# FFN in groups of up to four units, with q and k transposed together: a fused retention and FFN kernel on one core

## The chip, the core and the metric

The kernel runs on one core of a Trainium2 chip. The core has a matrix engine (TensorE, in the profile PE, its weight loads PEld), a vector engine (DVE), an activation engine (ACT), GpSimd (POOL) and a sync engine (SP) that issues DMAs here. Each engine works through its own instructions in order and waits on semaphores for the others. The metric is the device time of one execution in microseconds, as the median of several runs.

## What is computed

Eight batches of eight heads, 576 positions of 64 numbers. Scores are scaled, multiplied by a causal decay of each head, and applied to v; the result of all heads is one row of 512 per token, which goes through an FFN of 512 to 2048 to 512 with a squared ReLU.

```python
scores = scale * np.matmul(q, k.transpose(0, 1, 3, 2))
gamma = 1.0 - 2.0 ** (-5.0 - np.arange(H, dtype=np.float32))
rel = pos[:, None] - pos[None, :]
Dmat = np.where(rel >= 0, gamma[:, None, None] ** rel[None, :, :], 0.0)
ret = scores * Dmat[None, :, :, :]
attn_out = np.matmul(ret, v).astype(np.float32)
x = np.ascontiguousarray(attn_out.transpose(0, 2, 1, 3)).reshape(B * S, H * D)
h = x @ w_in
r = np.maximum(h, 0.0)
out = ((r * r) @ w_out).astype(np.float32)
```

## The kernel before

The tokens are cut into 36 units of 128. A full unit is 128 positions of one batch; a tail unit holds the last 64 positions of two batches. Each unit goes through two stages.

The retention stage (`add_ret`) casts k, q and v to fp16 (k and v on POOL, q on DVE for the first four units and on POOL after that; v is multiplied by its decay into `vp`). PE transposes k and q into one PSUM tile `psT` (line 307): four transposes for the k part (`tk`), four for q (`tq`). ACT copies the two halves of k out into `kTb` (`fe0`, line 316, and `fe1`, line 319), DVE copies q into `qT` (line 323). PE makes the scores `psc` (line 375), DVE masks them into `rT` (line 383). The state of earlier chunks, `R`, is made from `psS` (line 336) by DVE (`stmp`, line 350, then `R`, line 355, with the decay `bdec`). PE adds the two contributions into `psO` (lines 407 and 411), and DVE multiplies by the decay `gam` into `xT` (line 423).

The FFN stage (`add_ff`) multiplies `xT` by w_in: 16 output blocks of four accumulating matmuls, each with 128 moving columns (line 441, called FF1 below), four blocks to a PSUM bank `ph`. ACT takes the ReLU of a bank into `rl` (line 450), DVE squares it into `gT` (line 455). Sixteen accumulating matmuls with 512 moving columns then give `po` (line 466, FF2), which ACT copies out to `o` (line 474) and stores.

The order is not written out by hand. `Schedule` is a planner: each task has an engine, a key (smaller goes first among those that are ready), an estimated duration, the tasks it needs and the buffers it takes. `emit` plays the tasks through in the planner's own time and emits the instructions in the order that comes out. Constants are built ahead of it, so on DVE and POOL they stand before every task. The planner counts two banks for `ph` and one for `po`; both come from one pool of three.

Loads come from SP in one chain: k, q, v of units 0 to 3, then w_in and w_out in four pieces of 1 MB each (five stage buffers), then k, q, v of the other units. Each weight piece is cast in halves, one on DVE and one on ACT (line 256). The five load buffers of k, q and v are freed by the casts.

Of the kernel before, what the change touches and what calls it, by code (L numbers as in the profile page):

```python
# [97 lines left out]
def kernel(  # L98
# [26 lines left out]

    const = ctx.enter_context(tc.tile_pool(name="const", bufs=1))
    ld = ctx.enter_context(tc.tile_pool(name="ld", bufs=5))
    stage = ctx.enter_context(tc.tile_pool(name="stage", bufs=5))
# [26 lines left out]
    for h in range(H):  # L155
        nc.vector.memset(lnrow[:, h:h + 1], -lng[h])
    lncol = const.tile([P, NP], FP32, name="lncol")
# [3 lines left out]
    lnscale = const.tile([P, 1], FP32, name="lnscale")  # L161
    nc.vector.memset(lnscale, math.log(scale))

    mask = {}
    for kind in ("full", "tail"):
# [5 lines left out]
    nc.gpsimd.memset(mask["tail"][0:64, 64:128], 0.0)  # L171

    iota_pt = const.tile([P, 1], FP32, name="iota_pt")
    nc.vector.tensor_copy(out=iota_pt[0:64], in_=iota_p[0:64])
    nc.vector.tensor_scalar(out=iota_pt[64:128], in0=iota_p[64:128], scalar1=-64.0, scalar2=None, op0=ALU.add)
    vdec = {}
    for kind, pos in (("full", iota_p), ("tail", iota_pt)):
        t = const.tile([P, H], FP32, name=f"vdl_{kind}")
        nc.vector.tensor_scalar(out=t, in0=lnrow, scalar1=pos, scalar2=None, op0=ALU.mult)
        d = const.tile([P, H], FP32, name=f"vdec_{kind}")  # L180
        nc.scalar.activation(out=d, in_=t, func=ACTF.Exp, bias=lnscale, scale=1.0)
        vdec[kind] = d
    gam_f = const.tile([P, NP, P], FP32, name="gam_full")
    gam_t = const.tile([P, NP, P], FP32, name="gam_tail")
    for hp in range(NP):
        nc.scalar.activation(out=gam_f[:, hp, :], in_=iota_f, func=ACTF.Exp, scale=lncol[:, hp:hp + 1])  # L186
    nc.vector.tensor_copy(out=gam_t[:, :, 0:64], in_=gam_f[:, :, 0:64])
    nc.vector.tensor_copy(out=gam_t[:, :, 64:128], in_=gam_f[:, :, 0:64])
    gam = {"full": gam_f, "tail": gam_t}

    bdec = const.tile([P, NP, P], FP32, name="bdec")
    nc.vector.memset(bdec, 0.0)
    for hp in range(NP):
        nc.vector.memset(bdec[0:64, hp, 0:64], math.exp(128.0 * lng[2 * hp]))
        nc.vector.memset(bdec[64:128, hp, 64:128], math.exp(128.0 * lng[2 * hp + 1]))
# [299 lines left out]
    for u in range(NU):  # L495
        add_ff(u)
# [31 lines left out]
```

## Time and profile before

| | |
|---|---|
| median of 3 runs | 355.31 us (353.95 to 356.13) |
| the profiled execution | 354.32 us |
| its span | 352.6 us |
| instructions in the span | 9372 |
| PE matmul busy | 325.5 us (92%), 4000 matmuls |
| PE weight load busy | 250.7 us (71%) |
| DVE busy | 192.4 us (55%) |
| ACT busy | 155.3 us (44%) |
| POOL busy | 83.3 us (24%) |
| HBM read, written | 36.70 MB, 9.44 MB |

Busy time is the time that an engine's instructions cover. A matmul's busy time runs until its modelled end, so matmuls that follow each other overlap in the table of groups, and the spacing of their starts is what they cost in a stream. The profile's slices show the span in 40 parts, each digit a busy share in tenths. The timeline merges like instructions that follow each other; its columns are start, duration, engine, line, operation, and in brackets the idle time before it with what ended it. A row of the DMA slices and of the stretches gives the mean share of 16 DMA engines.

### The profile page before, as it was taken

How to read it: one execution, taken by the hardware profiler on the slowest of the kernel's cores; microseconds unless marked ns; L12 is line 12 of the kernel's file. 1: busy time of each engine (PE TensorE's matmuls, PEld its weight loads, DVE VectorE, ACT ScalarE, POOL GpSimd, SP SyncE). 2: the span in 40 equal slices, each digit the busy share in tenths (PEclk: the TensorE clock that was granted, in tenths of full speed). 3: DMA queues.
4: the chain of work that ended last, by engine and by line, in shares of the span. 5: the costliest groups of instructions: out<-in, count | busy, mean ns of one | idle time of the engine just before them, and what ended most of it. 6: DMA issues, size and time to landing. Idle time of an engine off the chain costs nothing.

```text
span 352.6 us, 9372 instructions
## 1 busy us (share of the span) xinstructions
PE 325.5 (92%) x4000; PEld 250.7 (71%) x4000; DVE 192.4 (55%) x400; ACT 155.3 (44%) x267; POOL 83.3 (24%) x117
## 2 busy tenths in 40 slices
PE   0479999999999999999999999999999999999994
PEld 0478857777777777777777777777777777777772
DVE  5689635554455555555455555555455555555440
ACT  3137843444434444444444444444444444444441
POOL 4400264422222222223122222222122222100000
PEclk9999999999999999999999999999999999999999
DMA  9999999998955444444445454555521000000001
GB/s 173 235 387 386 271 232 235 237 211 181 219 137 120 111 109 115 119 122 121 121 121 121 119 121 121 122 121 122 120 61 32 32 32 32 30 32 33 32 32 31
DMA packets 122026, 46.75 MB, mean 133 GB/s; under 512 B 113280, under 2 KB 113280, under 8 KB 121984
## 3 DMA queue, kind: packets, MB, share of 16 engines
q1 hardware_dynamic: 116736, 36.71, 45.4%
q10 hardware_dynamic: 5248, 9.44, 8.2%
q8 instruction: 31, 0.51, 0.6%
q14 instruction: 11, 0.09, 0.1%
HBM read 36.70 MB, written 9.44 MB: 131 GB/s over the span
## 4 chain that ended last, share of the span: by engine, by line
PE 86%; ACT 6%; DVE 4%; issue 1%; DVEq 0%
PE ph L441 34%; PE po L466 33%; PE psT L307 6%; ACT kTb L316 5%; PE psc L375 5%; PE psO L407 5%; PE psS L336 2%; PE psO L411 2%; DVE stmp L350 1%; DVE rT L383 1%; DVE w_in L256 0%; DVE R L355 0%; ACT kTb L319 0%; ACT gam_full L186 0%; DVE kTb L206 0%
## 5 line engine op out<-in xcount | busy, mean ns | idle before, releaser
L441 PE MATMUL ph<-xT,w_in 128*128 128x128 f16 x2304 | 158.3, 219 | 0.7 <-DVE w_in L256 0.7
L466 PE MATMUL po<-w_out,gT 128*128 128x512 f16 x576 | 155.0, 379 | 0.0
L441 PEld LDWEIGHTS <-w_in 128*128 128x128 f16 x2304 | 139.4, 98 | 9.6 <-DVE w_in L256 1.1
L450 ACT ACTIVATE rl<-ph 128x512 f16<-128x512 f32 x144 | 85.3, 596 | 53.5 <-PE ph L441 53.3
L455 DVE TENSOR_TENSOR gT<-rl 128x512 f16<-128x512 f16 x144 | 65.3, 456 | 37.6 <-ACT rl L450 37.2
L466 PEld LDWEIGHTS <-gT 128*128 128x128 f16 x576 | 53.3, 98 | 36.3
L474 ACT COPY o<-po 128x512 f32<-128x512 f32 x36 | 21.1, 586 | 97.2 <-PE po L466 93.9
L283 POOL CAST q<-q 128x512 f16<-128x512 f32 x32 | 19.8, 619 | 103.8 <-PE psT L307 60.0
L383 DVE TENSOR_TENSOR rT<-psc,mask_full 128x512 f16<-128x512 f32 x64 | 41.2, 682 | 4.3 <-PE psc L375 4.3
L288 POOL TENSOR_TENSOR vp<-v,vdec_full 128x512 f16<-128x512 f32 x32 | 34.2, 1069 | 36.2 <-PE psO L411 23.7
L407 PEld LDWEIGHTS <-vp 128*128 128x128 f16 x288 | 28.2, 100 | 19.3 <-issue 0.4
L375 PE MATMUL psc<-qT,kTb 128*128 128x128 f16 x288 | 38.4, 226 | 1.7 <-DVE qT L323 1.7
L279 POOL CAST k<-k 128x512 f16<-128x512 f32 x36 | 23.3, 647 | 70.5 <-DMA k<-in_k_dram 31.6
L407 PE MATMUL psO<-rT,vp 128*128 128x128 f16 x288 | 39.5, 224 | 0.0
L350 DVE TENSOR_TENSOR stmp<-psS,R 128x512 f32<-128x512 f32 x24 | 16.6, 690 | 38.4 <-PE psS L336 38.4
L423 DVE TENSOR_TENSOR xT<-psO,gam_full 128x512 f16<-128x512 f32 x32 | 22.1, 691 | 21.5 <-PE psO L411 18.0
L323 DVE COPY qT<-psT 128x512 f16<-128x512 f16 x36 | 15.3, 424 | 31.6 <-ACT rl L450 27.5
L319 ACT COPY kTb<-psT 64x512 f16<-64x512 f16 x36 | 20.9, 580 | 20.5 <-DVE qT L323 15.2
L316 ACT COPY kTb<-psT 64x512 f16<-64x512 f16 x36 | 20.8, 578 | 20.6 <-PE psT L307 20.1
L307 PEld LDWEIGHTS <-q 128*128 128x128 f16 x144 | 11.2, 99 | 24.2 <-issue 17.5
L307 PE MATMUL psT<-ident,q 128*128 128x128 f16 x144 | 14.4, 224 | 14.8 <-ACT kTb L316 6.8
L411 PE MATMUL psO<-qT,R 128*128 128x128 f16 (+1 forms) x128 | 24.7, 215 | 0.0
(49 smaller groups left out, 144.0 us busy)
## 6 DMA issues: line engine op xcount, KB each, us to landing
k<-in_k_dram SPq DMA_DIRECT2D x32, 256.0 KB, 4.4
q<-in_q_dram SPq DMA_DIRECT2D x32, 256.0 KB, 4.7
v<-in_v_dram SPq DMA_DIRECT2D x32, 256.0 KB, 3.3
out_dram<-o ACTq DMA_DIRECT2D x32, 256.0 KB, 2.7
wi<-in_moe_w_in_dram SPq DMA_DIRECT2D x4, 1024.0 KB, 9.4
wo<-in_moe_w_out_dram SPq DMA_DIRECT2D x4, 1024.0 KB, 8.0
k<-in_k_dram SPq DMA_DIRECT2D x8, 128.0 KB, 4.3
q<-in_q_dram SPq DMA_DIRECT2D x8, 128.0 KB, 4.2
```

The costliest lines, as they stand in the source:

```text
L279: nc.gpsimd.tensor_copy(out=t, in_=tile_of["k32", u].rearrange("p h d -> p (h d)"))
L288: nc.gpsimd.tensor_tensor(out=vo, in0=tile_of["v32", u].rearrange("p (n a) d -> p n a d", a=2), in1=vdec[kind].rearrange("p (n a o) -> p n ...
L307: nc.tensor.transpose(tile_of["psT", u][:, i, hp, :], tile_of[src, u][:, hp * P:(hp + 1) * P], ident)
L316: nc.scalar.copy(out=kT[0:64, :, 0, :], in_=tile_of["psT", u][0:64, 0])
L375: nc.tensor.matmul(tile_of["psc", u, half][:, j, a, :], lhsT=kT[:, hp, a, :], rhs=tile_of["qT", u][:, hp, :], start=True, stop=True)
L383: nc.vector.tensor_tensor(out=tile_of["rT", u][:, 2 * half:2 * half + 2].rearrange("p n a i -> p (n a) i"), in0=tile_of["psc", u, half].re ...
L407: nc.tensor.matmul(ps[:, hp, :], lhsT=vps[u % NB][:, hp, a * 64:a * 64 + P], rhs=tile_of["rT", u][:, hp, a, :], start=(a == 0), stop=(a == ...
L411: nc.tensor.matmul(ps[:, hp, lo:hi], lhsT=tile_of["R", ru][:, hp, :], rhs=tile_of["qT", u][:, hp, lo:hi], start=False, stop=(n == len(inte ...
L441: nc.tensor.matmul(tile_of["ph", u, fb][:, j, :], lhsT=w_in16[:, m, fi * P:(fi + 1) * P], rhs=tile_of["x", u][:, m, :], start=(m == 0), st ...
L450: nc.scalar.activation(out=t, in_=tile_of["ph", u, fb], func=ACTF.Relu)
L455: nc.vector.tensor_tensor(out=t, in0=rl, in1=rl, op=ALU.mult)
L466: nc.tensor.matmul(tile_of["po", u], lhsT=tile_of["g", u, fi // 4][:, fi % 4, :], rhs=w_out16[:, fi, :], start=(fi == 0), stop=(fi == NF - 1))
```

## The change

It has five parts.

- FFN groups. The units are put into groups of 1, 1, 2, then seven of 4, then 2, 1, 1. A group of n units has one `xT` of n x 128 columns. FF1 runs once for a group, with n x 128 moving columns; a `ph` bank then holds 4/n output blocks. FF2 stays one unit at a time. FF1 of a group needs the `xT` part of its last unit. `gT` has 32 buffers instead of 16, `xT` three instead of five.
- Transposes. q's transposes have the key just behind k's. From unit 4 on both wait for both casts and share `psT`; the ACT copies wait for q's transposes, the second ACT copy for the first, and DVE's `qT` for the second ACT copy. For the first four units q's transposes go to a bank of the score pool instead.
- Constants as tasks. `bdec` is filled on POOL from an ACT exponential instead of on DVE. Zeroing of the buffer sets 1 to 3 of `vp` and `kTb`, and the mask, positions and decay of the tail units, move from DVE and the start to POOL tasks; DVE zeroes set 0 alone.
- TensorE is warmed up: a first task of 40 matmuls of the identity with itself.
- FFN banks. `ph` and `po` share a count of three banks. Four weight stage buffers instead of five. Two latencies and some durations of the planner have new numbers.

The core of the diff:

```diff
-    LAT = {"PE": 0.25, "ACT": 0.12, "DVE": 0.12, "POOL": 0.15, "SP": 2.0}
+    LAT = {"PE": 0.25, "ACT": 0.12, "DVE": 0.12, "POOL": 0.12, "SP": 2.1}
...
+    sizes = [1, 1, 2] + [4] * 7 + [2, 1, 1]
...
-    stage = ctx.enter_context(tc.tile_pool(name="stage", bufs=5))
+    stage = ctx.enter_context(tc.tile_pool(name="stage", bufs=4))
...
-    x_pool = ctx.enter_context(tc.tile_pool(name="x", bufs=5))
+    x_pool = ctx.enter_context(tc.tile_pool(name="x", bufs=3))
-    g_pool = ctx.enter_context(tc.tile_pool(name="g", bufs=16))
+    g_pool = ctx.enter_context(tc.tile_pool(name="g", bufs=32))
...
-    sched = Schedule(dict(ph=2, po=1, psc=2, psT=1, psS=1, psO=1, ld=5, wst=5, k16=4, q16=4,
-                          qT=3, rT=3, x=5, g=4, rl=3, o=2, R=6))
+    sched = Schedule(dict(ff=3, psc=2, psT=1, psS=1, psO=1, ld=5, wst=4, k16=4, q16=4,
+                          qT=3, rT=3, x=3, rl=3, o=2, R=6))
...
+    def warm():
+        ps = ps_ff.tile([P, P], FP32, name="warm", tag="ff")
+        for _ in range(40):
+            nc.tensor.matmul(ps, lhsT=ident, rhs=ident, start=True, stop=True)
+    add("PE", -1000, 5.5, warm)
+    zeroed = [[]]
+    for i in range(1, NB):
+        zeroed.append([add("POOL", -6 * L + L * i, 0.8, lambda i=i: (zero_kT(nc.gpsimd, i), zero_vp(nc.gpsimd, i)))])
+    def make_bdec():
+        nc.gpsimd.memset(bdec, 0.0)
+        for lo in (0, 64):
+            nc.gpsimd.tensor_copy(
+                out=bdec[lo:lo + 64, :, lo:lo + 64],
+                in_=dec128[lo:lo + 64].rearrange("p (n o) -> p n o", o=1).to_broadcast([64, NP, 64]))
+    made_bdec = add("POOL", -6 * L + 1, 1.1, make_bdec)
+    def make_tail_pool():
+        make_mask("tail")
...
+    tail_pool = add("POOL", 0, 2.2, make_tail_pool, deps=[made_bdec])
+    tail_dec = add("DVE", 0, 0.3, lambda: make_vdec("tail", tile_of["iota_pt"]), deps=[tail_pool])
...
-        tk = add("PE", base - 17.6, 0.22, ft(0, "k16"), deps=[ck], acq=("psT",))
-        tq = add("PE", base - 15.6, 0.22, ft(1, "q16"), deps=[cq, tk])
+        tk = add("PE", base - 17.6, 0.22, ft(0, "k16"), deps=[ck] if early else [ck, cq], acq=("psT",))
+        tq = add("PE", base - 17.5, 0.22, ft(1, "q16"), deps=[cq, tk], acq=("psc",) if early else ())
...
-        e0 = add("ACT", base - 15.5, 0.58, fe0, deps=[tk] + prev)
-        e1 = add("ACT", base - 15.4, 0.58, fe1, deps=[tk] + prev)
-        eq = add("DVE", base - 15.3, 0.42, feq, deps=[tq], acq=("qT",))
+        e0 = add("ACT", base - 15.5, 0.58, fe0, deps=[tk if early else tq] + prev)
+        e1 = add("ACT", base - 15.4, 0.58, fe1, deps=[e0])
+        eq = add("DVE", base - 15.3, 0.42, feq, deps=[tq] if early else [tq, e1], acq=("qT",))
...
-                        nc.tensor.matmul(tile_of["ph", u, fb][:, j, :], lhsT=w_in16[:, m, fi * P:(fi + 1) * P],
-                                         rhs=tile_of["x", u][:, m, :], start=(m == 0), stop=(m == NP - 1))
+                        nc.tensor.matmul(tile_of["ph", g, fb][:, j, :], lhsT=w_in16[:, m, fi * P:(fi + 1) * P],
+                                         rhs=tile_of["x", us[0]][:, m, :], start=(m == 0), stop=(m == NP - 1))
```

How the order changes at three places. First POOL at the start, where `k` is the fp16 cast of a unit's k and `vp` its v. Before:

```order
L167 MEMSET mask_full 128x128
L168 AFFINE_SELECT mask_full<-mask_full 128x128
L167 MEMSET mask_tail 128x128
L168 AFFINE_SELECT mask_tail<-mask_tail 128x128
L171 MEMSET mask_tail 64x64
L279 CAST k_189<-k_183 128x512
L288 TENSOR_TENSOR vp_163<-v_187,vdec_full 128x4x2x64
```

After, the rows from the end of the third buffer set on; ahead of them stand the mask, `bdec` and the first two sets:

```order
L207 MEMSET kTb_149 64x4x128
L208 MEMSET kTb_149 64x4x128
L204 MEMSET vp_145 128x4x64
L186 MEMSET mask_tail 128x128
L187 AFFINE_SELECT mask_tail<-mask_tail 128x128
L243 MEMSET mask_tail 64x64
L245 COPY iota_pt<-iota_p 64x1
L246 TENSOR_SCALAR iota_pt<-iota_p 64x1
L248 COPY gam_tail<-gam_full 128x4x64
L249 COPY gam_tail<-gam_full 128x4x64
L318 CAST k_226<-k_197 128x512
L327 TENSOR_TENSOR vp_142<-v_210,vdec_full 128x4x2x64
```

The first k cast moves behind all of POOL's constants. The second place is PE in the middle of the program, where one unit's k and q are transposed. Before:

```order
L307 MATMUL psT<-ident,k_984 128x128
L441 LDWEIGHTS w_in_96
L441 MATMUL ph<-xT,w_in_96 128x128
L441 LDWEIGHTS w_in_96
L441 MATMUL ph<-xT,w_in_96 128x128
L441 LDWEIGHTS w_in_96
L441 MATMUL ph<-xT,w_in_96 128x128
L441 LDWEIGHTS w_in_96
L441 MATMUL ph<-xT,w_in_96 128x128
L466 LDWEIGHTS gT
L466 MATMUL po<-w_out_97,gT 128x512
L307 LDWEIGHTS q_1014
```

After:

```order
L530 MATMUL po<-w_out_97,gT 128x512
L351 LDWEIGHTS k_1644
L351 MATMUL psT<-ident,k_1644 128x128
L351 LDWEIGHTS k_1644
L351 MATMUL psT<-ident,k_1644 128x128
L351 LDWEIGHTS k_1644
L351 MATMUL psT<-ident,k_1644 128x128
L351 LDWEIGHTS k_1644
L351 MATMUL psT<-ident,k_1644 128x128
L351 LDWEIGHTS q_1576
L351 MATMUL psT<-ident,q_1576 128x128
```

Four FF1 matmuls and one FF2 matmul stood between the two; now nothing does. The third place is ACT in the same stretch, where `kTb` are the two copies of k and `rl` a ReLU of FF1. Before:

```order
L474 COPY o<-po 128x512
L480 DMA out_dram<-o 128x512
L450 ACTIVATE rl<-ph 128x512 x3
L316 COPY kTb_180<-psT 64x4x128
L450 ACTIVATE rl<-ph 128x512
L319 COPY kTb_180<-psT 64x4x128
```

After:

```order
L511 ACTIVATE rl<-ph 128x512 x4
L357 COPY kTb_147<-psT 64x4x128
L360 COPY kTb_147<-psT 64x4x128
L511 ACTIVATE rl<-ph 128x512 x8
L357 COPY kTb_148<-psT 64x4x128
L360 COPY kTb_148<-psT 64x4x128
L511 ACTIVATE rl<-ph 128x512 x4
```

The ReLUs come sixteen to a group of four units, with the copies of two units between them, and the copies of the other two units fall into the group's FF2.

More of the change, by code (lines that the diff above doesn't have):

```diff
@@ L170 @@
         mask[kind] = m
[L171 to L182, printed above, removed]
+    make_mask("full")
@@ L270 @@
     T = {}
-    L = 2 * NF
     def add_ret(u):
         kind, b, c = units[u]
-        base = (u - 1) * L
+        us = groups[group_of[u]]
+        base = (u - len(us)) * L
+        early = u < ahead
+        tail = [tail_pool, tail_dec] if kind == "tail" else []
         def fk():
@@ L425, in add_ret, with add_ff @@
+        T["x", u] = add("DVE", base + 22.6, 0.7, fx, deps=[outs[-1]] + ([T["x", u - 1]] if s else []),
+                        acq=() if s else ("x",))
         sched.free("psO", [T["x", u]])
         T["out", u] = outs[-1]
-    def add_ff(u):
-        kind, b, c = units[u]
-        base = u * L
+    T["ff2"] = []
+    def add_ff(g):
+        us = groups[g]
+        n = len(us)
+        base = us[0] * L
+        nf = 4 // n
         f1 = []
         sq = []
-        for fb in range(4):
-            for j in range(4):
+        done = g - 1
+        while done >= 0 and sum(4 * len(groups[i]) for i in range(done, g + 1)) <= 32:
+            done -= 1
+        before = [T["ff2"][done]] if done >= 0 else []
+        for fb in range(NF // nf):
+            for j in range(nf):
@@ L490 @@
+        T["ff2"].append(f2[-1])
     for u in range(NU):
```

182 lines of the change are left out of this document (105 added, 77 removed).

## The prediction

> **What bounds the kernel now.** I read the page first (busy slices, chain, groups), then the stretches, then the waits, then the timeline at three places: the start, one middle unit, the end.
>
> ```profile
> PE   0479999999999999999999999999999999999994
> DVE  5689635554455555555455555555455555555440
> ...
> 20.00:27.15 7.15, 4.82 (x55) 4.41 (x55) 6.68 (x13) 2.74 (x4) 0.00 (x0) 1.00 1.05 387
> 27.15:45.00 17.85, 17.58 (x268) 15.64 (x269) 13.80 (x26) 14.89 (x22) 2.77 (x3) 1.00 1.05 322
> 45.00:345.00 300.00, 293.16 (x3610) 223.53 (x3609) 159.32 (x308) 131.21 (x229) 71.21 (x93) 1.00 0.47 112
> ```
>
> The columns of a stretch are its length and the busy time of PE, weight load, DVE, ACT and POOL, then clock, DMA share and GB/s. From 27 us on PE is the bound; from 20 to 27 us it is DVE, busy 6.68 of 7.15 us. What PE costs when nothing holds it is read at the end, where the last unit runs alone:
>
> ```profile
> 340.59 3.74 PE L441 MATMUL ph<-xT,w_in 128*128 128x128 f16 x64
> 344.16 3.62 PE L466 MATMUL po<-w_out,gT 128*128 128x512 f16 x16
> ```
>
> The 64 narrow matmuls take from 340.59 to 344.16, 55.8 ns each. The 16 wide ones end with one of 0.38 us, so (3.62 - 0.38)/15 = 216 ns from start to start. All else on PE is 128 wide and goes at 55.8 ns. What holds PE in the middle is one wait, once in a unit:
>
> ```profile
> 71.61 0.39 PE L307 MATMUL psT<-ident,k 128*128 128x128 f16 x4
> 72.03 0.58 ACT L316 COPY kTb<-psT 64x512 f16<-64x512 f16 x1 [0.30 <-PE psT L307]
> 72.05 0.38 PE L466 MATMUL po<-w_out,gT 128*128 128x512 f16 x1
> 72.51 0.59 ACT L450 ACTIVATE rl<-ph 128x512 f16<-128x512 f32 x1
> 72.66 0.38 PE L307 MATMUL psT<-ident,q 128*128 128x128 f16 x4 [0.23 <-ACT kTb L316]
> ...
> PE psT L307 <- ACT kTb L316: 6.8, 30, 0.2
> ```
>
> The q transposes stand one wide matmul after the k transposes, but start only when ACT has copied the first half of psT (72.03 + 0.58 = 72.61). The wide matmul started at 72.05 and the next start is 72.66: 0.61 us where 0.216 would do. The view shows 0.23 of it as idle, since the modelled end of the matmul covers the rest. It happens 30 times: 30 x 0.39 = 11.7 us.
>
> **The transposes side by side (saves 11.7 us).** q's transposes now follow k's at once, before any reader of psT, so there is nothing to wait for. What the copies wait for is later by four matmuls, 0.22 us. The DVE copy of qT now waits for both ACT copies, 2 x 0.58 us; behind it on DVE stand one or two squares gT, and three rl buffers lie between those and ACT. The score matmuls that need qT stand several ph matmuls later. The pair now waits for the later of two POOL casts; POOL is busy 71.21 of 300 us, so I cost that at nothing, and if the cover fails it is the third rival. Bounds: 0 to 11.7.
>
> **Wide FFN matmuls (saves 3.4 us).** 28 of 36 units lie in groups of four: 28 x 16 = 448 times, four narrow matmuls (4 x 55.8 = 223 ns) become one of 216: 448 x 7.2 ns = 3.2 us. In the two groups of two, 128 pairs (112 ns) become matmuls of 256 columns, which no row has. They lie between half a wide one (108) and the pair (112): 0 to 0.5 us; I take the middle, 0.2. The Trainium skill (TensorE: Matmul & The Clock Gate, Back-to-back issue gap) has columns/2.4 + 2.5 ns, which agrees with both measured spacings; by it a pair costs 109 ns and this term is 0.3.
>
> ACT and DVE do the same 144 relus and squares of 128x512. In a group of four 16 relus come in a row, one per 4 x 0.216 = 0.86 us, and take 0.60 each (the row at 72.51). Two kT copies between them make ACT late by at most 2 x 0.58 - (0.86 - 0.60) = 0.9 us. PE's lead is three banks, 2.6 us, less fill, hop and relu (0.86 + 0.2 + 0.6), so 0.9, and the transposes that precede the copies keep PE off the banks for 0.45 more. I cost it at nothing; if the lead is short by the 0.45, two such places in seven groups make 6 us, which is kept for the range. FF2's two groups use the same bank order as now. The next group's first matmul needs the x of the group's last unit: behind its last psO stand 12 wide matmuls, 2.6 us, against a drain of 0.2, one DVE operation of 0.6 and xT of 0.7; margin 1.1 us.
>
> **The start (saves 2.6 us).** The rows that carry it:
>
> ```profile
> 1.59 0.20 POOL L167 MEMSET mask_full<- 128x128 f32 x1
> 2.78 0.14 POOL L171 MEMSET mask_tail<- 64x64 f32 x1
> 2.87 1.26 ACT L186 ACTIVATE gam_full<-iota_f,lncol 128x128 f32<-128x128 f32 x4
> 4.21 0.71 POOL L279 CAST k<-k 128x512 f16<-128x512 f32 x1 [1.29 <-DMA k<-in_k_dram]
> 4.97 0.61 PE L307 MATMUL psT<-ident,k 128*128 128x128 f16 x4 [4.97 <-POOL k L279]
> 10.43 0.35 DVE L283 CAST q<-q 128x512 f16<-128x512 f32 x1
> 11.63 0.60 POOL L279 CAST k<-k 128x512 f16<-128x512 f32 x1
> 12.11 0.42 DVE L323 COPY qT<-psT 128x512 f16<-128x512 f16 x1 [1.32 <-ACT kTb L319]
> 13.89 1.04 POOL L288 TENSOR_TENSOR vp<-v,vdec_full 128x512 f16<-128x512 f32 x1 [1.65 <-DMA v<-in_v_dram]
> 25.46 0.42 DVE L323 COPY qT<-psT 128x512 f16<-128x512 f16 x1
> 25.81 0.68 DVE L350 TENSOR_TENSOR stmp<-psS,R 128x512 f32<-128x512 f32 x1
> 26.40 0.68 DVE L256 CAST w_in<-wi 128x1024 f16<-128x1024 f32 x1
> 27.15 2.85 PE L441 MATMUL ph<-xT,w_in 128*128 128x128 f16 x48 [0.45 <-DVE w_in L256]
> 34.51 1.96 PE L441 MATMUL ph<-xT,w_in 128*128 128x128 f16 x32 [0.27 <-DVE w_in L256]
> ```
>
> Before, DVE's constants delay the first q cast to 10.43, and the first FFN matmul waits until 27.15 for DVE's half of w_in. After, DVE is free early, but POOL does the zeroing, bdec and the tail constants ahead of its first k cast. Its rows give 0.20 us for 128 elements and 0.14 for 64; the line through them gives 0.56 for 512 and 0.32 for 256, and start to start I take 0.5 and 0.3. From the mask at 2.1: bdec's copies wait for ACT (gam_full 1.26 plus one more activation, about 4.0) and end about 4.7; three buffer sets at 0.5 + 0.5 + 0.3 make 8.6; the tail's mask, positions and two copies (half a cast each, in all 1.8) make 10.4. So the first k cast goes from 4.21 to 10.4. With the cast (0.6) and eight transposes on the slow clock, qT of unit 0 is at 12.15, as now.
>
> From there to DVE's w_in cast I walked DVE's new order: until xT of unit 0 the chain PE-ACT-DVE sets the time (3.7 us: 15.85, now 15.50). Then stmp waits for psS until 16.6, and from there DVE is full: nine operations of 0.60 from start to start (25.81 to 26.40) and four of 0.35 (25.46 to 25.81), and twice 0.1 where R needs the end of its stmp, so 7.0 us: the cast is at 23.6 and ends at 24.3 instead of 27.1. The gain is that q's transposes no longer wait for k's copies there (separate bank). PE has the same work behind it at that point (three units and unit 3 up to its scores), so 2.85 us are won. Then the second w_in cast stands three DVE operations later (24.3 + 4 x 0.6): PE waits 0.6 us; the old wait of 0.4 ahead of 34.51 goes. Net 2.6.
>
> The bounds: POOL's 512-element memset between 0.4 (the slope of 64 elements) and 0.8 (four times 128 elements) puts the k cast at 8.3 to 13.2, the first FFN matmul at 22.7 to 27.1: a gain of 0 to 4. The upper end is capped by the loads:
>
> ```profile
> 53.57 0.61 POOL L283 CAST q<-q 128x512 f16<-128x512 f32 x1 [0.28 <-DMA q<-in_q_dram]
> ```
>
> Unit 7's q lands at 53.5, behind the weights, and the first group of four needs its x: cast, transposes, two ACT copies, qT, scores, two masks, psO and xT add 0.6 + 0.65 + 1.2 + 0.4 + 0.6 + 1.3 + 0.5 + 0.7, so 59.5. PE runs out of other work at 24.3 + 0.6 + 14.1 (FF1 of units 0 to 3) + 13.8 (FF2) + 8.5 (scores and outputs of units 3 to 8) = 61.3. So this is late next: with 1.8 us more won it decides. Four stage buffers instead of five hold wo back until w_in's first cast; three w_in transfers are under way then, and SP has only loads behind it that queued there before too, so nothing. The 40 warm-up matmuls run from about 1.4 us, where PE idles until 4.97: nothing.
>
> What they bring is a matter of the clock:
>
> ```profile
> 24.98 0.38 PE L307 MATMUL psT<-ident,q 128*128 128x128 f16 x4 [1.26 <-ACT kTb L319]
> ...
> 347.80:351.00 3.20, 0.00 (x0) 0.00 (x0) 0.00 (x0) 0.58 (x1) 0.00 (x0) 1.00 0.37 82
> 351.40:352.60 1.20, 0.00 (x0) 0.00 (x0) 0.00 (x0) 0.00 (x0) 0.00 (x0) 0.50 0.03 7
> ```
>
> Four transposes take 0.61 at 4.97 and 0.38 at 24.98: the start runs at half clock. At the end the clock falls to 0.50 between 351.0 and 351.4, some 3.5 us after the last matmul (344.16 + 3.62). The warm-up ends near 5.7 and POOL lets the next matmul come near 11, so the clock is down again and I count no gain. The Trainium skill (TensorE: Matmul & The Clock Gate, What's actually happening) says the same against this part: one idle window of about 3.4 us returns the array to half clock; the trace agrees, with its 3.5.
>
> **The sum.** The profiled execution took 354.32 us (span 352.6, 1.7 around it). 354.32 - 11.7 - 3.4 - 2.6 = 336.6. The median of the runs shown is 1.0 above that execution, so 337.6.
>
> **Rivals.** (1) POOL's constants cost more than I put and the start wins nothing or loses up to 2 us: 340 to 342. For it: no long POOL memset is in the trace. Against: they overlap loads anyway. (2) The clock stays up from the warm-up, because POOL is faster: some 30 matmuls on the chain are 50 ns shorter, 1.5 us, and the loads cap the sum at 1.8: 336. Against: the row at 351.40. (3) The transposes still wait, now for POOL's q cast, so that part does nothing: 337.6 + 11.7 = 349.3. For it: the casts follow each other on POOL. Against: POOL idles three quarters. (4) Slower: the groups' first matmul waits for the last unit's x. Margin 1.1 us; it decides from 17.7/7 = 2.5 us per group of four, an x 3.6 us late, six relus' worth. At 6 us late it gives 337.6 + 7 x 4.9 = 372. Against: the last unit's attention runs beside FF2, where ACT has only the output copies.
>
> **How the numbers follow.** As forecast 0.74; (1) 0.12; (2) 0.05; (3) 0.05; (4) 0.04. The forecast is 337.6; upward its range takes in stalls of 6 us in FF1 (343.6), downward the start's 4 us instead of 2.6, the clock's 1.5 and the 1.1 by which the runs shown stray from their median (333.6). So 333.5 to 343.5. That takes in (1) and (2) and holds 0.85 or so. About 1% is what a measurement of this kernel can tell from no change: faster by more than that (below 351.8) is everything but (4): 0.94 with a little off for causes not seen; within 1% 0.03; slower 0.03.
>
> **What would show it.** Right: no wait of PE at L351 for ACT in the middle; ph in groups of four at 216 ns; POOL's first k cast near 10.4 and the first FFN matmul near 24.3; 0.61 for four transposes at 11 us. Wrong: idle PE ahead of a group's first ph, or of ph inside a group on ACT; a first FFN matmul after 27; the end is unchanged, 4.8 us behind the last matmul.

## The result and the profile after

The changed kernel takes 339.94 us (median of 4 runs, 339.76 to 340.7); the kernel before, run beside it, 355.15 (4 runs, 353.95 to 356.13). The ratio is 0.9577, with a 95% interval of 0.9544 to 0.9611. That is 15.2 us less, where 17.7 were forecast; the time lies inside the range.

The page of the changed kernel, profiled in an execution of 339.76 us. Its first rows are the span and the busy time of each engine:

```profile
span 338.0 us, 6569 instructions
PE 322.6 (95%) x2568; PEld 197.0 (58%) x2568; DVE 198.9 (59%) x378; ACT 157.1 (46%) x268; POOL 89.6 (27%) x133
```

PE has 1432 matmuls fewer: the 2304 narrow ph matmuls have become 832 of three widths, and the 40 of the warm-up are new. The groups, with shapes kept apart (count, then busy us and mean ns of one, then idle time ahead):

```profile
L503 PE MATMUL ph<-xT,w_in 128*128 128x512 f16 x448 | 108.4, 379 | 0.0
L503 PE MATMUL ph<-xT,w_in 128*128 128x128 f16 x256 | 16.0, 219 | 0.4 <-DVE w_in L293 0.4
L503 PE MATMUL ph<-xT,w_in 128*128 128x256 f16 x128 | 15.1, 273 | 0.0
```

What a matmul of 256 columns costs in a stream is read from one run of 16 of them:

```profile
38.50 1.91 PE L503 MATMUL ph<-xT,w_in 128*128 128x256 f16 x16
```

With 0.273 for the last, (1.91 - 0.273)/15 = 109 ns from start to start; the trace's starts behind 66 us have a mean of 109.2, and of 215.9 at 512 columns.

PE's waits in the changed kernel: who waits, for whom, how long in all, how often, and the longest:

```profile
PE psT L351 <- POOL k L318: 5.7, 1, 5.7
PE psTq L351 <- DVE rT L432: 1.6, 2, 1.2
...
PE psT L351 <- POOL q L322: 0.8, 2, 0.6
PE psTq L351 <- DVE q L322: 0.7, 1, 0.7
```

The row of 30 waits for ACT's copy of kT is gone. The rows of psTq are new: in the start, q's transposes now take a score bank, and wait until DVE has read it, or for DVE's q cast. The stretches of the changed kernel (length; busy PE, weight load, DVE, ACT, POOL; clock, DMA share, GB/s):

```profile
45.00:66.00 21.00, 20.17 (x202) 13.38 (x201) 16.49 (x27) 8.77 (x16) 11.39 (x16) 1.00 1.12 229
66.00:330.00 264.00, 264.00 (x1984) 152.12 (x1983) 152.43 (x278) 123.27 (x212) 61.41 (x79) 1.00 0.47 109
```

The same stretches of the kernel before:

```profile
45.00:66.00 21.00, 20.77 (x207) 13.85 (x206) 9.56 (x19) 8.76 (x16) 11.60 (x15) 1.00 1.10 234
66.00:330.00 264.00, 257.39 (x3220) 198.31 (x3218) 144.29 (x278) 116.50 (x203) 59.61 (x79) 1.00 0.44 106
```

From 66 us on PE is never idle now. Ahead of 66 us it is worse than before: 0.83 us idle between 45 and 66 instead of 0.23. Where the 14.6 us of span (352.6 to 338.0) came from, by the starts of the matmuls:

| part | forecast us | measured us | how |
|---|---|---|---|
| transposes side by side | 11.7 | 11.7 | all 30 waits gone, 0.39 each |
| wide FFN matmuls | 3.4 | 3.6 | 448 x (4 x 55.8 - 215.9 = 7.3 ns) = 3.3; 128 x (2 x 55.8 - 109.2 = 2.4 ns) = 0.3 |
| start, up to 66 us | 2.6 | -1.1 | first FFN matmul at 26.29 instead of 27.15: +0.86; lost behind it to 45 us 0.91 instead of 0.46, at w_in: -0.45; new waits at 53 to 65 us: -1.48 |
| behind the last matmul | 0 | 0.4 | the last one ends at 347.78 of 352.6 before, at 333.55 of 338.0 after: 4.8 and 4.4 |

The table's sum is 14.6. So three terms held and one did not: the start lost 1.1 us instead of winning 2.6. Its rows in the changed kernel's timeline (start, length, and in brackets the idle time ahead and who ended it):

```profile
2.11 0.52 POOL L234 MEMSET bdec<- 128x512 f32 x1
...
5.24 0.71 DVE L322 CAST q<-q 128x512 f16<-128x512 f32 x1 [1.88 <-DMA q<-in_q_dram]
5.62 0.58 POOL L204 MEMSET vp<- 128x256 f16 x1
7.29 0.30 POOL L204 MEMSET vp<- 128x256 f16 x1
10.86 0.61 POOL L318 CAST k<-k 128x512 f16<-128x512 f32 x1
11.53 0.61 PE L351 MATMUL psT<-ident,k 128*128 128x128 f16 x4 [5.65 <-POOL k L318]
14.55 1.04 POOL L327 TENSOR_TENSOR vp<-v,vdec_full 128x512 f16<-128x512 f32 x1
14.55 1.32 DVE L322 CAST q<-q 128x512 f16<-128x512 f32 x1
17.22 0.69 DVE L475 TENSOR_TENSOR xT<-psO,gam_full 128x512 f16<-128x512 f32 x1 [0.22 <-PE psO L456]
18.50 0.42 DVE L322 CAST q<-q 128x512 f16<-128x512 f32 x1
25.49 0.68 DVE L293 CAST w_in<-wi 128x1024 f16<-128x1024 f32 x1
26.29 1.95 PE L503 MATMUL ph<-xT,w_in 128*128 128x128 f16 x32
28.63 2.19 PE L503 MATMUL ph<-xT,w_in 128*128 128x128 f16 x32 [0.39 <-DVE w_in L293]
...
61.12 0.61 POOL L322 CAST q<-q 128x512 f16<-128x512 f32 x1 [2.21 <-DMA q<-in_q_dram]
61.79 0.40 PE L351 MATMUL psT<-ident,q 128*128 128x128 f16 x4 [0.18 <-POOL q L322]
64.06 0.69 DVE L475 TENSOR_TENSOR xT<-psO,gam_full 128x512 f16<-128x512 f32 x1 [0.19 <-PE psO L460]
65.33 0.40 PE L351 MATMUL psT<-ident,q 128*128 128x128 f16 x4 [0.58 <-POOL q L322]
65.56 0.81 PE L503 MATMUL ph<-xT,w_in 128*128 128x512 f16 x3
```

POOL's k cast came at 10.86 (10.4 forecast). Unit 1's q cast on DVE took 1.32 us beside POOL's vp (14.55 to 15.59); alone it takes 0.42. xT of unit 0 came at 17.22 instead of 15.85, DVE's w_in cast at 25.49 instead of 23.6. Then, at 61 and 65 us, q's transposes of units 8 and 9 wait for a load and its cast, and the first group of four begins at 65.56, right behind them.

The loads themselves also came later than before. With four stage buffers, w_out's first transfer waited for w_in's first cast and was issued at 26.24 us, where the kernel before issued it at 16.54. The DMA share, the second figure from the end, fell there (the changed kernel first, then the kernel before):

```profile
26.00:28.00 2.00, 2.00 (x40) 2.00 (x37) 2.00 (x5) 0.62 (x2) 0.00 (x0) 1.00 0.76 273
26.00:28.00 2.00, 1.55 (x29) 1.38 (x27) 2.00 (x4) 0.00 (x0) 0.00 (x0) 1.00 1.05 388
```

Unit 4's k cast came at 42.70 instead of 41.41, unit 7's q cast at 54.51 instead of 53.57.

### The profile page after: what moved, and what is told of

Its sections match the earlier page's. It is cut to its first block, busy times and chain, and to the rows that moved or that the text cites. A ratio compares the mean times of both kernels' runs of the same rounds, so it can differ in the third digit from the quotient of the medians.

```text
span 338.0 us, 6569 instructions
## 1 busy us (share of the span) xinstructions
PE 322.6 (95%) x2568; PEld 197.0 (58%) x2568; DVE 198.9 (59%) x378; ACT 157.1 (46%) x268; POOL 89.6 (27%) x133
## 4 chain that ended last, share of the span: by engine, by line
PE 88%; DMA 4%; POOL 3%; ACT 2%; DVE 2%; issue 0%; SPq 0%; POOLq 0%
PE ph L503 37%; PE po L530 35%; PE psO L456 4%; PE psc L424 4%; PE psT L351 4%; PE psS L385 2%; PE psO L460 2%; DMA q<-in_q_dram 1%; DMA out_dram<-o 1%; DMA k<-in_k_dram 1%; DVE rT L432 1%; DVE q L322 0%; POOL kTb L208 0%; POOL kTb L207 0%; POOL k L318 0%
## 5 line engine op out<-in xcount | busy, mean ns | idle before, releaser
L530 PE MATMUL po<-w_out,gT 128*128 128x512 f16 x576 | 149.6, 379 | 0.0
L503 PE MATMUL ph<-xT,w_in 128*128 128x512 f16 (+2 forms) x832 | 139.0, 313 | 0.4 <-DVE w_in L293 0.4
L516 DVE TENSOR_TENSOR gT<-rl 128x512 f16<-128x512 f16 x144 | 70.4, 494 | 37.3 <-ACT rl L511 35.5
L503 PEld LDWEIGHTS <-w_in 128*128 128x128 f16 x832 | 68.0, 98 | 40.2 <-DVE w_in L293 0.6
L537 ACT COPY o<-po 128x512 f32<-128x512 f32 x36 | 21.1, 586 | 55.8 <-PE po L530 55.4
L318 POOL CAST k<-k 128x512 f16<-128x512 f32 x36 | 23.2, 645 | 62.7 <-DMA k<-in_k_dram 24.7
L456 PEld LDWEIGHTS <-vp 128*128 128x128 f16 x288 | 26.5, 100 | 16.6
L456 PE MATMUL psO<-rT,vp 128*128 128x128 f16 x288 | 35.5, 224 | 0.0
L364 DVE COPY qT<-psT 128x512 f16<-128x512 f16 x32 | 13.6, 424 | 36.5 <-ACT kTb L360 36.3
L424 PEld LDWEIGHTS <-kTb 128*128 128x128 f16 x288 | 24.8, 102 | 15.8 <-ACT kTb L360 1.0
L424 PE MATMUL psc<-qT,kTb 128*128 128x128 f16 x288 | 33.2, 226 | 0.5 <-DVE qT L364 0.3
L351 PE MATMUL psT<-ident,k 128*128 128x128 f16 x144 | 14.9, 229 | 5.7 <-POOL k L318 5.7
```

The costliest lines, as they stand in the source:

```text
L318: nc.gpsimd.tensor_copy(out=t, in_=tile_of["k32", u].rearrange("p h d -> p (h d)"))
L351: nc.tensor.transpose(tile_of["ps" + src[0], u][:, i, hp, :], tile_of[src, u][:, hp * P:(hp + 1) * P], ident)
L424: nc.tensor.matmul(tile_of["psc", u, half][:, j, a, :], lhsT=kT[:, hp, a, :], rhs=tile_of["qT", u][:, hp, :], start=True, stop=True)
L456: nc.tensor.matmul(ps[:, hp, :], lhsT=vps[u % NB][:, hp, a * 64:a * 64 + P], rhs=tile_of["rT", u][:, hp, a, :], start=(a == 0), stop=(a == ...
L503: nc.tensor.matmul(tile_of["ph", g, fb][:, j, :], lhsT=w_in16[:, m, fi * P:(fi + 1) * P], rhs=tile_of["x", us[0]][:, m, :], start=(m == 0) ...
L516: nc.vector.tensor_tensor(out=t, in0=rl, in1=rl, op=ALU.mult)
```

## The experiments

All are the changed kernel with an edit, but the first, which is the kernel before with an edit. Times are medians; the ratio is to the kernel before, whose medians beside them were 353.99 to 355.15. An interval of a ratio is 1.0 to 1.7 us to either side, so differences of an us between two of them rest on rows, not on times alone.

| run | us | ratio, 95% interval |
|---|---|---|
| the change | 339.94 | 0.9577, 0.9544 to 0.9611 |
| e1 transposes alone | 343.63 | 0.9693, 0.9659 to 0.9727 |
| e2 groups of one | 341.47 | 0.9627, 0.9590 to 0.9664 |
| e3 no warm-up | 339.90 | 0.9584, 0.9535 to 0.9633 |
| e4 early k | 338.61 | 0.9551, 0.9521 to 0.9581 |
| e5 pairs, then fours | 338.71 | 0.9544, 0.9510 to 0.9577 |
| e6 = e4 + e5 | 337.69 | 0.9517, 0.9485 to 0.9548 |
| e7 two banks + one | 340.58 | 0.9595, 0.9557 to 0.9634 |
| e8 long warm-up, three of four runs | 339.71 | 0.9573, 0.9530 to 0.9615 |
| e9 q casts on ACT | 338.79 | 0.9545, 0.9510 to 0.9580 |
| e10 = e6 + loads told | 335.52 | 0.9452, 0.9423 to 0.9482 |
| e11 = e10 + e9 | 336.23 | 0.9469, 0.9438 to 0.9500 |
| e12 loads told alone | 341.23 | 0.9649, 0.9620 to 0.9677 |

### One part alone, one part undone

**e1: the kernel before with the transposes side by side, and nothing else.**

```diff
-        tk = add("PE", base - 17.6, 0.22, ft(0, "k16"), deps=[ck], acq=("psT",))
-        tq = add("PE", base - 15.6, 0.22, ft(1, "q16"), deps=[cq, tk])
+        early = u < ahead
+        tk = add("PE", base - 17.6, 0.22, ft(0, "k16"), deps=[ck] if early else [ck, cq], acq=("psT",))
+        tq = add("PE", base - (15.6 if early else 17.5), 0.22, ft(1, "q16"), deps=[cq, tk])
...
+        e0 = add("ACT", base - 15.5, 0.58, fe0, deps=[tk if early else tq] + prev)
+        e1 = add("ACT", base - 15.4, 0.58, fe1, deps=[tk] + prev if early else [e0])
+        eq = add("DVE", base - 15.3, 0.42, feq, deps=[tq] if early else [tq, e1], acq=("qT",))
```

> The kernel before, with q's transposes behind k's and both ACT copies and qT in a row from unit 4 on; nothing else is changed. Theory (the 30 waits of 0.39 us were the copy of k holding psT): all 30 go, nothing takes their place, 355.2 - 11.7 = 343.5 (343 to 344.5). Rival (the wait only moves, to POOL's q cast or to DVE's qT behind the second ACT copy): 350 or more, with PE idle ahead of the transposes or the scores.

It took 343.63 us, 11.0 less than its 354.59 of before. The stretch and a unit of it:

```profile
66.00:330.00 264.00, 264.00 (x3342) 206.26 (x3341) 147.74 (x287) 119.51 (x208) 60.05 (x79) 1.00 0.45 108
```

```profile
72.38 0.39 PE L307 MATMUL psT<-ident,k 128*128 128x128 f16 x4
72.60 0.39 PE L307 MATMUL psT<-ident,q 128*128 128x128 f16 x4
```

q's transposes start 0.22 us behind k's, with narrow FFN matmuls on all sides, and PE is busy 264.00 of 264.00. This part alone makes the middle free of waits; nothing it hides comes up in place of the 30 waits. What is missing of the 11.7 lies at the start: in this profile the clock came up at 28.7 us instead of 23.7, and the first FFN matmul at 27.93 instead of 27.15.

**e2: groups of one unit throughout,** the other parts kept.

```diff
-    sizes = [1, 1, 2] + [4] * 7 + [2, 1, 1]
+    sizes = [1] * 36
```

> The changed kernel with 36 groups of one unit, so FF1 is 128 columns wide again. Theory (the wide FF1 saves 448 x 7.4 ns + 128 x 2.4 ns = 3.6 us, and the group of four is what waits for the loads of units 7 to 9, 1.2 us): 340 + 3.6 - 1.2 = 342.4 (341.8 to 344). Rival (the groups give back at the start all that they save): 340.5 or less.

341.47 us, a little under the range expected. What the wide matmuls win (3.6) is gone, but so is a loss: the stretch from 45 to 66 us is full.

```profile
45.00:66.00 21.00, 21.00 (x197) 13.56 (x196) 9.46 (x17) 8.11 (x14) 10.86 (x15) 1.00 0.98 229
```

By the starts of the matmuls PE loses 1.7 us less ahead of 66 us than in the changed kernel. So the groups of four win 3.6 us and cost 1.7 where loads are late.

**e3: no warm-up.**

```diff
-    add("PE", -1000, 5.5, warm)
```

> The changed kernel without the 40 warm-up matmuls. Theory (the clock is at half speed either way until about 24 us, and PE had nothing else to do until 11.5): 339.9, within 0.6. Rival (the warm-up makes the clock come up earlier): 341 to 342, with four transposes still at 0.61 us later than 24.1 us.

339.90 us: the warm-up is worth nothing that can be measured. The four runs lie further apart than others, 338.01 to 341.58. In the profiled one, the fastest, the clock came up early all the same, at 15.2 us, as the lengths of four transposes show:

```profile
11.54 0.61 PE L350 MATMUL psT<-ident,k 128*128 128x128 f16 x4 [11.54 <-POOL k L317]
15.95 0.40 PE L350 MATMUL psTq<-ident,q 128*128 128x128 f16 x4 [0.66 <-DVE q L321]
```

Its first FFN matmul is at 25.17, 1.1 us ahead of the changed kernel's, with the same order at the start.

### Where the start went

**e4: the first k cast early.** The zeroing of buffer sets 1 to 3 goes to DVE, the tail constants behind the first four units' loads.

```diff
-        zeroed.append([add("POOL", -6 * L + L * i, 0.8, lambda i=i: (zero_kT(nc.gpsimd, i), zero_vp(nc.gpsimd, i)))])
+        zeroed.append([add("DVE", -6 * L + L * i, 0.87, lambda i=i: (zero_kT(nc.vector, i), zero_vp(nc.vector, i)))])
...
-    tail_pool = add("POOL", 0, 2.2, make_tail_pool, deps=[made_bdec])
+    tail_pool = add("POOL", 0, 2.2, make_tail_pool, deps=[made_bdec, loaded["v", ahead - 1]])
```

> The changed kernel with buffer sets 1 to 3 zeroed on DVE instead of POOL, and the tail's constants on POOL only after unit 3's v has been loaded, so POOL's first k cast does not stand behind them. Theory (POOL's constants set the start, and behind that the loads): k cast near 4.8 us instead of 10.9, first FFN matmul near 21.5 us instead of 26.3 (bound by the landing of w_in), but the first group of four still waits for the loads and starts near 63 to 65, so of 4.8 us earlier at most 1.5 are left: 338.5 to 340. Rival A (DVE's own work or the slow clock sets the start): first FFN matmul at 25 to 26.5 all the same. Rival B (no cap by the loads): 335 to 336.

338.61 us. Its rows:

```profile
4.71 0.61 POOL L318 CAST k<-k 128x512 f16<-128x512 f32 x1
21.57 1.67 PE L503 MATMUL ph<-xT,w_in 128*128 128x128 f16 x13
25.06 1.85 PE L503 MATMUL ph<-xT,w_in 128*128 128x128 f16 x30 [0.28 <-ACT w_in L291]
...
55.96 0.40 PE L351 MATMUL psT<-ident,q 128*128 128x128 f16 x4 [0.59 <-POOL q L322]
61.39 0.40 PE L351 MATMUL psT<-ident,q 128*128 128x128 f16 x4 [1.26 <-POOL q L322]
```

The k cast is 6.2 us earlier (4.71 instead of 10.86) and the first FFN matmul 4.7 (21.57 instead of 26.29), but the time falls by 1.3 only. By the starts of the matmuls PE loses 2.0 us more than in the changed kernel ahead of 45 us, since the clock is low until 23.2 and FFN matmuls wait for casts of w_in and w_out. It loses 1.7 more between 45 and 66, most of it at 56 and 61 us, where PE waits for q of units that have only just landed. So POOL's constants do set the start, and the weights and loads set what it is worth. The clock may have a part in the 4.7, since here it was up from 6.1 to 19.8 us.

**e5: two more pairs ahead of the fours,** so that the first group of four comes later.

```diff
-    sizes = [1, 1, 2] + [4] * 7 + [2, 1, 1]
+    sizes = [1, 1, 2, 2, 2] + [4] * 6 + [2, 1, 1]
```

> The changed kernel with groups of 1, 1, 2, 2, 2, then six of 4: units 4 to 7 no longer wait for each other, the start is untouched. Theory (at the first group of four PE waits 1.4 us for loads; pairs have work earlier and cost 0.16 us more in FF1): first FFN matmul still near 26.3, waits between 45 and 66 us gone, 339.9 - 1.2 = 338.7 (338.2 to 339.3). Rival (the waits only come from the transposes of units that are not loaded yet, whatever the groups): 339.9 or a little more.

338.71 us, with the first FFN matmul at 26.43, as in the changed kernel. PE idles 0.20 us between 45 and 66, where the changed kernel had 0.83. A pair needs two units' x, not four, so FFN work is there while loads are late.

**e6: e4 and e5 together.**

> The early k casts of the fourth experiment together with the pairs of the fifth. Theory (the earlier start and the loads' cap hide each other's gain): first FFN matmul near 21.6, waits at 55 to 62 us shorter, about 2.7 us below the early k casts alone: 336 (335.2 to 337). Rival (the loads cap both alike): 338.4 or more.

337.69 us, above the range expected, though not as high as the rival. One wait was left, as long as in e4:

```profile
60.27 0.40 PE L351 MATMUL psT<-ident,q 128*128 128x128 f16 x4 [1.27 <-POOL q L322]
```

FFN matmuls of a pair, whose x was there from 55.6 on, ran up to 58.6 and went on only at 60.62, behind the transposes. That the planner put these ahead because it prices each load at 1.2 us, and so takes q to have landed, is what e12 and e10 try. In the changed kernel the k casts of units 4 to 7 come 1.2 us per load apart (42.70 to 53.46 in nine loads), but those of 8 and 9 come 1.6 and 1.8 per load apart.

**e9: q casts of the first four units on ACT,** away from POOL's vp.

```diff
-            (nc.vector if early else nc.gpsimd).tensor_copy(
+            (nc.scalar.copy if early else nc.gpsimd.tensor_copy)(
...
-            cq = add("DVE", base - L, 0.42, fq, deps=[loaded["q", u]], acq=("q16",))
+            cq = add("ACT", base - L, 0.6, fq, deps=[loaded["q", u]], acq=("q16",))
```

> The changed kernel with the q casts of units 0 to 3 on ACT instead of DVE. Theory (behind the late k cast DVE's row of work sets the first FFN matmul, and its second q cast, 1.32 us while POOL writes vp, is part of it): 1.3 + 0.4 + 0.4 us leave that row, the first FFN matmul comes near 24.3 instead of 26.3; behind it the loads keep half or more: 339.2 (338.5 to 340). Rival (PE's slow transposes and ACT's copies set it, and ACT only gets later): first FFN matmul at 26 or later, 340 to 341.

338.79 us, as expected, but the first FFN matmul came at 25.13, not at 24.3:

```profile
25.13 1.96 PE L503 MATMUL ph<-xT,w_in 128*128 128x128 f16 x32 [0.90 <-DVE w_in L293]
```

In this profile PE's clock came up at 17.7 us, in the changed kernel's at 23.9. In e3 and e12 it came up at 15.2 and 15.0, and their first FFN matmuls are at 25.17 and 25.21 with the casts still on DVE. So the 1.2 us cannot be put down to the casts; an earlier clock gives as much. The casts did leave DVE free: unit 0's qT copy to its xT took 3.64 us (12.33 to 15.97) instead of 4.62 (12.60 to 17.22). But the planner then put one rT and one stmp more ahead of the w_in cast, which came at 24.39, as in e3 (24.37). The intervals of the ratios of e9 and the change overlap.

**e12: only the planner told of the loads,** 1.5 us for each from unit 4 on, in place of 1.2.

```diff
-            loaded[name, u] = dma_task(0, 1.2 if loaded else 2.1, fn, acq=("ld",) if n == 0 else ())
+            loaded[name, u] = dma_task(0, (1.2 if u < 4 else 1.5) if loaded else 2.1, fn, acq=("ld",) if n == 0 else ())
```

> The changed kernel, groups and constants as they are, with the planner told 1.5 us instead of 1.2 for each load from unit 4 on. Theory (the wait at 61 to 65 us is transposes of units 8 and 9 that the plan put ahead of the first group of four, because it believed the loads faster): first FFN matmul unchanged near 26.3, the 1.4 us of waits between 45 and 66 us gone or below 0.4, 339.9 - 1.2 = 338.7 (338.2 to 339.3). Rival (the first group of four lacks its own last x there): 339.7 or more, PE idle ahead of the first wide ph.

341.23 us: the theory fell. The intervals of this one and of the change do not meet, so it is slower. The first FFN matmul came at 25.21 (its clock came up for good at 15.0), but PE then idles 2.38 us between 45 and 66, in place of 0.83. That is not for late loads: w_out's first transfer went out at 25.16 here, the DMA share from 26 to 28 us was 1.03, and unit 4's k cast came at 41.39, as before the change. The waits ahead of the first group of four, whose FF1 is the third row:

```profile
62.20 0.61 PE L424 MATMUL psc<-qT,kTb 128*128 128x128 f16 x8 [1.08 <-DVE qT L364]
64.03 0.27 PE L456 MATMUL psO<-rT,vp 128*128 128x128 f16 x2 [0.78 <-DVE rT L432]
65.91 3.61 PE L503 MATMUL ph<-xT,w_in 128*128 128x512 f16 x16 [0.32 <-DVE xT L475]
```

Now PE waits for unit 7's own attention instead of for the transposes of units 8 and 9. The first group of four needs x of unit 7, and behind the FFN of units 0 to 3 little else is there. The planner now takes unit 7 to be later than it is: its q cast ended at 54.97 and its transposes began only at 59.21, 4.2 us later; in the changed kernel it was 2.6. So a price of 1.5 is too high for unit 7, and the wait moves and grows. Whether another order would fill this place with fours was not tried.

**e10: e6 with the planner told of the loads;** the edits are those of e4, e5 and e12.

> The early k casts and the pairs, with the planner told 1.5 us instead of 1.2 for each load from unit 4 on; only the order changes. Theory (what is left of the wait at the loads is transposes of units not yet loaded that stand ahead of FFN work that is ready): the 1.7 us of waits at 58 to 61 us go, 337.7 - 1.6 = 336.1 (335.5 to 336.8). Rival (PE has no other work there, the loads cap it in any order): 337.3 or more, the wait elsewhere.

335.52 us (4 runs, 335.41 to 335.87), as expected, and faster than both kernels: 0.9452, with an interval of 0.9423 to 0.9482 against the change's 0.9544 to 0.9611. Its stretch:

```profile
45.00:66.00 21.00, 21.00 (x207) 15.71 (x205) 13.92 (x26) 11.41 (x21) 11.08 (x15) 1.00 1.08 229
```

The three edits are worth 1.3, 1.2 and -1.3 us one at a time by the medians (0.9, 1.2 and -2.6 by the ratios), and 4.4 together by either. e6 has 2.2 of them, and telling the planner wins the other 2.2 on top of e6, where alone it lost. The reading that fits: the early k gives PE its FFN work sooner, the pairs keep some of it in reach at 55 to 65 us, and with a higher price for a load the planner puts it there. Pairs with the loads told, without the early k, were not run.

**e11: e10 with e9.**

> The tenth experiment with the q casts of units 0 to 3 on ACT too. Theory (with early k casts the landing of w_in sets the first FFN matmul, not DVE): as the tenth, within 0.5. Rival (DVE still counts): 1 us or more below it.

336.23 us, 0.7 above e10, a little more than expected, and inside its interval. The first FFN matmul is at 21.60 (21.64 in e10): with the k cast early, the casts on DVE are not what the start waits for.

### Banks and the clock

**e7: the FFN's three shared banks made two for ph and one for po,** as before the change.

```diff
-    sched = Schedule(dict(ff=3, psc=2, psT=1, psS=1, psO=1, ld=5, wst=4, k16=4, q16=4,
+    sched = Schedule(dict(ph=2, po=1, psc=2, psT=1, psS=1, psO=1, ld=5, wst=4, k16=4, q16=4,
```

> The changed kernel with two banks counted for ph and one for po, as before the change. Theory (a fill of 0.86 us, a hop of 0.2, a ReLU of 0.6 and a hop of 0.1 make 1.76 us, and two banks allow 1.73, so every kT pair between ReLUs and every po in a row stops PE; one po bank costs 0.9 us at each of some 26 changes of unit inside a group unless other work fills it): 345 to 360. Rival (attention work fills the gaps, and the shared banks do not matter): 340 to 341.

340.58 us: the theory (345 to 360) fell, the rival was right. The stretch, two rows of a group of four, and the one wait that is left:

```profile
66.00:330.00 264.00, 263.21 (x1975) 151.44 (x1973) 149.40 (x277) 123.22 (x211) 60.34 (x79) 1.00 0.48 110
```

```profile
99.71 1.89 PE L503 MATMUL ph<-xT,w_in 128*128 128x512 f16 x8
101.44 0.28 PE L424 MATMUL psc<-qT,kTb 128*128 128x128 f16 x2
...
315.85 0.40 PE L503 MATMUL ph<-xT,w_in 128*128 128x128 f16 x4 [0.79 <-DVE xT L475]
```

With two banks PE idles 0.79 of 264 us, in place of none, and that is one wait for `xT` of a last unit at 315 us, not for a bank. Four wide matmuls fill a bank, so eight fill both, in 1.73 us. By the prediction's estimate the first is free again 0.86 + 0.2 + 0.6 = 1.66 after its start (fill, hop, relu): two banks just reach. Where they would not, since ACT has kT copies between, transposes, scores and outputs of other units stand between the ph matmuls. The median is 0.6 above the change, which the intervals do not separate.

**e8: 135 warm-up matmuls instead of 40.**

```diff
-        for _ in range(40):
+        for _ in range(135):
```

> The changed kernel with 135 warm-up matmuls instead of 40. If the clock comes up by 8 us, they end by 11.5, when the first k cast is done, and the transposes at 11.5 take 0.38 us for four; the first FFN matmul comes near 25.3 and of that 1 us a half is left behind the loads: 339.4. If the clock stays down whatever runs (as in the changed kernel's trace until 23.9), they end at 15.9 and the first FFN matmul comes 3 to 4 us later: 342 to 343.

339.71 us (the middle of three runs, 338.81 to 340.5), and no gain. That is near the 339.4 of a clock that comes up, and under the 342 to 343 of one that stays down. A fourth execution took 692.61 us. It is the profiled one, so where the clock came up in the others is not in a trace.

## Why the prediction was right

The mechanism and the direction were right, and the time lies in the range, 2.3 us above the figure. Against the profiled execution the forecast was 336.6 and 339.76 came.

**The transposes: right.** 11.7 forecast and measured; e1 gives 11.0 by its median with that part alone. The things named as its cover held: PE has no wait for qT, for the kT copies or for POOL's casts behind 66 us. Rival (3) is out by e1.

**Wide matmuls: right, 0.2 too little.** The 256 wide matmul, which no row of before had, goes at 109.2 ns from start to start; the bounds were 108 and 112. The Trainium skill (TensorE: Matmul & The Clock Gate, Back-to-back issue gap) gives columns/2.4 + 2.5 ns for a matmul by itself, which makes an estimate of 109.2, and the trace agrees. The same section gives about 81 and 131 ns for 128 and 512 columns in a real stream of weight loads and matmuls; here each matmul has its weight load, PE is busy 264.00 of 264.00 us, and the spacings are 55.8 and 215.9, so the measurement decides against those two.

**Groups of four: right.** No ph matmul in the middle waits for a bank, and no group for its last x; the 6 us kept for stalls in FF1 weren't needed. The margin was larger than the prediction's 0.9 us suggests: e7 takes a bank away, and behind 66 us still no ph matmul waits for one. The forecast counted as if the 64 wide matmuls of a group ran in a row; in the trace, attention work stands between them. Rival (4) is out: between 66 and 330 us PE is never idle. A group's lack of x does show, but at one place, the first group, while loads are late (e12).

**The start: the term that was mis-sized, +2.6 forecast, -1.1 measured.** Four steps of it:

- POOL's constants were sized rightly: 0.52 and 0.30 us (forecast 0.5 and 0.3) and the k cast at 10.86 (10.4). The bounds given for that cast, 8.3 and 13.2, do not follow from the 0.4 and 0.8 us they name: three buffer sets of 1.0 or of 2.0 us make 9.5 and 12.5.
- "Until xT of unit 0 the chain PE-ACT-DVE sets the time", priced at 3.7 us, left out that the q cast of unit 1 stands on DVE there. POOL's vp of unit 2 started in the same 14.55, and the cast took 1.32 us, 0.9 more than alone. In the kernel before, the same cast came at 15.08, behind a vp of 13.89 to 14.93, and took 0.41. So xT came 1.4 us late, 0.5 of it with the k cast and 0.9 in this chain, which took 4.62; in e9, with the cast on ACT, it took 3.64. The Trainium skill (SBUF — State Buffer, SBUF: two separate sides) says that GpSimd and a VectorE instruction in a two-port mode share a port pair, and that whichever starts first holds it for its whole instruction. The trace is near that: 15.59, where vp ends, and 0.35 for the cast of before make 15.94, and this one ended at 15.87.
- From there to the w_in cast the prediction walked DVE as full, 7.0 us from 16.6 to 23.6. The cast came at 25.49, 1.9 late. In e3 and e12, the same order with the clock up from 15.2 and 15.0 us, it came at 24.37 and 24.42, so some 1.1 of the 1.9 go with the clock: DVE waited for matmuls that ran slowly.
- "This is late next" at the loads was right in kind and wrong in time. The prediction has x of unit 7 at 59.5 and PE out of work at 61.3, so 1.8 us in hand; x was ready at 64.75. Of the 5.3 us, 1.0 is the q cast, which ended at 55.12 instead of 54.1. Another 2.6 passed before PE began unit 7's transposes at 57.72, behind work of other units, and the other 1.7 lie in the chain behind them. The prediction followed unit 7 as if no other unit stood in the queues, and it put four stage buffers instead of five at nothing, though the loads came some 1 us later with w_out's late issue. No run has the changed kernel with five buffers, so what the fifth is worth is open. PE lost 1.5 us there though the start had won only 0.9. e4 shows the cap plainly: 4.7 us won, 1.3 left.

**Warm-up: right,** as nothing (e3), though not by the argued reason alone, since the clock is not as regular as the prediction took it. Two of the changed kernel's four executions have a mean granted clock of 0.979, about what e7 has (0.977), where the clock rose early and fell back. They took 339.76 and 340.13 us, the two with 1.000 and 0.999 339.76 and 340.7.

**Rivals.** What came is rival (1) in its time (340 to 342, at its lower edge) but not in its cause: POOL's constants cost what was forecast. Rival (2), the clock staying up, was not seen in the profile of the changed kernel (four transposes take 0.61 us at 11.53). That the range held the time is in part luck: upward it was widened by 6 us for stalls in FF1, which did not come, and the start's loss used that room.

## What to carry to other kernels

Where an in-order engine stops once in a unit for a copy that frees a bank, put the work that follows next to what it waits behind: the whole wait times its count came back, and it could be read off the timeline beforehand. A gain at the start of a kernel is worth only what the next thing in line leaves, and that place must be walked with all units in the queues, not with the one unit alone. Where a planner sets the order, changing its price for a load helps only if there is ready work to put in its place: here three edits worth 1.3, 1.2 and -1.3 us alone made 4.4 together. Buffers given up at the start can delay what is loaded behind them, so look at the DMA share there.

## What the runs showed of the hardware

**The clock came up at different times for the same start.** Read from the records of the granted clock in the traces, with 40 warm-up matmuls: first up at 4.7 to 7.3 us in e4, e6, e7, e10, e11 and e12, at 17.7 in e9, at 23.7 to 24.5 in the change, e2 and e5; without any, at 15.2 in e3, 23.7 in the kernel before and 28.7 in e1. Ahead of the first record a stretch shows 1.00 whatever the clock is; there the lengths of the matmuls tell (0.61 us for four transposes at 11.53 in the changed kernel). In the first six it fell back after 3.4 to 13.7 us and rose again later, at about 15 us in e12 and between 22 and 26 in the others. The changes within one profile lie multiples of 3.41 us apart. So 4.4 us of dense matmuls raise the clock in some executions and not in others, and it does not stay up while the first units leave PE waiting. The Trainium skill (TensorE: Matmul & The Clock Gate, What's actually happening) has a free-running window of 3.4 us that decides; the 3.41 agree with it. A stretch of e7 (the clock is the third figure from the end) shows it low again after its early rise:

```profile
9.50:11.00 1.50, 0.00 (x0) 0.00 (x0) 0.45 (x1) 0.30 (x1) 1.31 (x7) 0.50 1.35 217
```

**One whole execution at half pace.** e8's profiled execution, with more warm-up than any other, ran its matmuls at half the usual pace from start to end. Its busy row and its po group:

```profile
PE 683.2 (99%) x2663; PEld 335.5 (49%) x2663; DVE 196.7 (28%) x378; ACT 159.5 (23%) x268; POOL 88.9 (13%) x133
...
L530 PE MATMUL po<-w_out,gT 128*128 128x512 f16 x576 | 305.3, 677 | 0.0
```

A po matmul takes 677 ns in place of 379, while DVE, ACT and POOL are as busy as ever in us (196.7, 159.5, 88.9). It is not the half clock of the other starts. There the warm-up matmuls start 107 ns apart, each like the next; here they start mostly 56 and 166 ns apart by turns, so they go at the full pace with a pause behind every first or second one. Matmuls of 512 columns start 443 ns apart, at times some 555, in place of 216. The trace of that execution has no clock record at all. Why it ran so was not found.

**POOL and DVE hold each other up both ways.** POOL's 256 element memset took 0.58 us at 5.62, beside DVE's q cast of 5.24 to 5.95, and 0.30 at 7.29, alone; DVE's cast took 1.32 beside vp, and 0.42 at 18.50. In the kernel before, unit 1's q cast on DVE and a k cast on POOL both started at 15.08: DVE's took 0.41, POOL's 0.88 in place of 0.60. The prediction had priced each engine's constants as if it were alone.
